# An FFT convolution with a SiLU feed-forward layer on one core: the inverse first stage as two half sums in four column quarters

## The chip, the cores and the metric

The kernel runs on one core of a Trainium2 chip, as one launch. The metric is the device time of that launch in microseconds (us). The core's engines have names of their own here: PE does the matmuls, PEld is its weight load, DVE, ACT and POOL do elementwise work, SP issues DMAs. PE writes to PSUM; DVE and ACT read PSUM or SBUF.

## The reference

Two functions follow each other. The first is a long causal convolution done by FFT, times its own input; the second is a feed-forward layer on each token.

```
h = (relu(pos_emb @ w1) @ w2) * exp(-0.01 * pos)[:, None]       # 12480 x 128
u = x * v                                                        # 2 x 12480 x 128
y = irfft(rfft(u, 24960) * rfft(h, 24960), 24960)[:, :12480]
a = x * y                                                        # tokens for the layer
g = a @ w_in;  g = g * sigmoid(g)                                # 24960 x 2048
out = g @ w_out                                                  # 24960 x 128
```

All inputs and outputs are f32.

## The kernel before

**The transform.** A sequence is taken as 2 x 98 x 64 positions: token 64 * (98 * i + t1) + t2, with i the half, t1 the slow index of 98 values and t2 the fast one of 64. The forward transform takes stage A over t1 (98 rows contracted against the constant `fa`) and stage B over t2 (`fb`, `fc`), two of the 98 values of k1 at a time. Products with the filter's spectrum follow, then the inverse of stage B, whose result `ws` goes to a DRAM tensor `wd`, as a real and an imaginary part for every k1 and t2. The inverse of stage A, which the change is about, is done in the second half of the kernel, tile by tile: y(t1, t2) is the sum over 98 values of k1 of real part times cosine and imaginary part times sine, with `fai` [98, 2, 98] as the constant.

**The stages in time.** The filter and batch 0 come first. Then the feed-forward loop runs over 52 token tiles. For its first 24 tiles batch 1 is transformed beside it, a side generator (`batch1_steps`) whose events the loop draws a few per step from a table of offsets; afterwards the loop runs alone.

**A token tile** is five values of t2 (the last tile of each half has four) with 97 or 98 values of t1 each, so 490, 486, 392 or 388 token columns. `load_tile` fetches the tile of `wd` (the two parts, 98 partitions) and the matching columns of x. `attn_tile` then does the inverse first stage. For each of the m values of t2, for both parts c and for both halves h of the 128 channels it issues one f32 matmul, which loads 64 columns of `wd` as weights and lets the 97 or 98 columns of `fai` pass (L656 to L665); the two parts accumulate in PSUM. DVE multiplies with x into `att` (L670), ACT rounds that to `ah` in the format fp32r (L671), DVE makes the rest `al` (L672). All matmuls of the layer use such pairs of a high and a low part, three products each.

**The loop** (L854 on) has 52 x 16 steps; a step is one block of 128 of the 2048 inner columns. On PE it does three hq matmuls (L861 to L863) and, for the step three before (LAG), three op matmuls (L889 to L891). Between lie silu on ACT (L868), gh on DVE or ACT (L870, L872) and gl on DVE (L873). hq has three PSUM buffers. While batch 1 runs beside, silu writes hq in place and gh and gl read it, so the buffer is free only after gl; later silu writes SBUF. The order on each engine is the order of the program text:

```
if f == 8 and n + 1 < len(tiles):
    attn[n + 1] = attn_tile(n + 1, *ahead.pop(n + 1), pmy, ("yp", 1))
if f == 9 and n + 2 < len(tiles):
    ahead[n + 2] = load_tile(n + 2)
while done < total and done * n_side < (s + 1) * total:
    done += next(side, total)
```

So in step 8 of a tile PE does the burst of L659 for the next tile, between hq of step 8 and op of step 5. ACT has ah and DVE has att and al in their queues between the work of steps 8 and 9. The burst's PSUM tile `yp` has one buffer and is written once per tile. Tile 0 is made ahead of the loop, with stage A groups of batch 1 around it (`seq3`, letter Y).

Of the kernel before, what the change touches and what calls it, by code (L numbers as in the profile page):

```python
# [10 lines left out]
F32 = mybir.dt.float32  # L11
# [3 lines left out]
ALU = mybir.AluOpType  # L15
# [8 lines left out]
D = 128  # L24
NJ = 64
DFF = 2048
R = 98
C = 64
T = R * C
N = 2 * T  # L30
NI = 2
NQ = R // 2
NF = DFF // 128


# [13 lines left out]
def tile_widths(i, n):  # L49

    if i == 0:
        return [98] * n
    w = [97] * n
    if n % 2:
        w[-1] = 98
    return w
# [28 lines left out]
def kernel(  # L85
# [17 lines left out]
    nc = tc.nc  # L103
# [9 lines left out]
    dram = dpool("dram")  # L113
    hs = dram.tile([NQ, 128, 512], F32, name="hs")
    wd = [dram.tile([R, NI, 128, D], F32, name=f"wd{b}") for b in range(NB)]

    const = pool("const")
    fa_sb = const.tile([R, 392], F32, name="fa_sb")
    fai_sb = const.tile([R, 2, R], F32, name="fai_sb")
    warm_sb = const.tile([1, 1], F32, name="warm_sb")  # L120
    win_sb = const.tile([R, 128], F32, name="win_sb")
    w1_sb = const.tile([128, 128], F32, name="w1_sb")
# [256 lines left out]
    for t in P["seq"]:  # L379
# [21 lines left out]
        elif t == "p":  # L401
            g = len(pts)
            pts.append(ppool.tile([128, NP, R], F32, name=f"pt{g}", tag="pt", bufs=8))
            for o in range(0, NP, 4) if g == 0 else [0]:
                n = 4 if g == 0 else NP
# [202 lines left out]

    for it in range(-1, NQ):
        if it + 4 < NQ:  # L610
            fbs[it + 4] = load_fb(rpa, it + 4, 7, nc.sync if it < 0 else nc.scalar, fc)
# [8 lines left out]
        if it >= 0:  # L620
            hab = habs.pop(it)
            at = products(it, up, hab[:, 1:2], "at", 3, nc.vector)
# [27 lines left out]
    def attn_tile(n, wt, xs, psp, tag):  # L650
        b, i, t2, m = tiles[n]
        ws = tile_widths(i, m)
        w = sum(ws)
        yp = psp.tile([128, 512], F32, name=f"yp{n}", tag=tag[0], bufs=tag[1])
        o = 0
        for t in range(m):  # L656
            for c in range(2):
                for h in range(0, D, 64):
                    nc.tensor.matmul(  # L659
                        yp[h : h + 64, o : o + ws[t]],  # L660
                        wt[:, c, t * D + h : t * D + h + 64],
                        fai_sb[:, c, 0 : ws[t]],
                        start=(c == 0),
                        stop=(c == 1),
                    )  # L665
            o += ws[t]
        at = mt.tile([128, 490], F32, name=f"att{n}", tag="att", bufs=1)
        ah = mt.tile([128, 512], F32R, name=f"ah{n}", tag="ah", bufs=2)
        al = mt.tile([128, 512], F32R, name=f"al{n}", tag="al", bufs=2)
        nc.vector.tensor_tensor(out=at[:, 0:w], in0=yp[:, 0:w], in1=xs[:, 0:w], op=ALU.mult)  # L670
        nc.scalar.copy(out=ah[:, 0:w], in_=at[:, 0:w])  # L671
        nc.vector.tensor_tensor(out=al[:, 0:w], in0=at[:, 0:w], in1=ah[:, 0:w].bitcast(F32), op=ALU.subtract)  # L672
        return ah, al
# [4 lines left out]
    for t in P["seq3"]:  # L678
# [13 lines left out]
        elif t == "U":  # L692
# [5 lines left out]
            mt = pool("mt")  # L698
# [31 lines left out]
    class Carved:  # L730


        at = dict(hab=(0,), at=(1024,), bt=(1792,), uw=(2560,), ws=(3072,), fb=(3584, 5868))
# [119 lines left out]
    op = {}  # L853
    for s in range(len(steps) + LAG):  # L854
        if s < len(steps):
            n, f = steps[s]
            w = sum(tile_widths(*tiles[n][1::2]))
# [7 lines left out]
            g = hp if beside else moe.tile([128, 490], F32, name=f"g{s}", tag="g", bufs=2)  # L865
# [15 lines left out]
        if s >= LAG:  # L881
            n, f = steps[s - LAG]
            w = sum(tile_widths(*tiles[n][1::2]))
            if f == 0:
                op[n] = pm.tile([128, 512], F32, name=f"op{n}", tag="op", bufs=2)
            o = op[n]
# [28 lines left out]
def _constants():  # L915
    k1 = np.arange(R, dtype=np.float64)
    t1 = np.arange(R, dtype=np.float64)
    t2 = np.arange(C, dtype=np.float64)
    k2 = np.arange(C, dtype=np.float64)
    phi = 2.0 * np.pi * np.outer(t1, k1 + 0.5) / 196.0  # L920
    alt = 1.0 - 2.0 * (np.arange(R) % 2)
    fa = np.concatenate([np.cos(phi), -np.sin(phi), alt * np.sin(phi), alt * np.cos(phi)], axis=1)
    fai = np.stack([np.cos(phi.T), -np.sin(phi.T)], axis=1) * (2.0 / N)
    th = 2.0 * np.pi * ((k1[:, None, None] + 0.5) / N + k2[None, None, :] / C) * t2[None, :, None]
    co, si = np.cos(th), np.sin(th)
    fwd = np.concatenate([np.concatenate([co, -si], axis=2), np.concatenate([si, co], axis=2)], axis=1)
    inv = fwd.transpose(0, 2, 1)
    fb = np.stack([fwd, inv], axis=1).reshape(NQ, 2, 2, 128, 128).transpose(0, 3, 1, 2, 4)
    rows_k2 = inv.reshape(NQ, 2, 2, 64, 128).transpose(0, 1, 3, 2, 4).reshape(NQ, 128, 2, 128)
    fc = np.stack([fwd.reshape(NQ, 2, 128, 128).transpose(0, 2, 1, 3), rows_k2], axis=2)  # L930
    pos = np.zeros(2 * T, np.float32)
    pos[:S] = np.arange(S, dtype=np.float32)
    win = np.exp(np.float32(-0.01) * pos)
    win = win.reshape(NI, R, C).transpose(1, 0, 2).reshape(R, 128)
    return {k: np.ascontiguousarray(a, dtype=np.float32) for k, a in dict(fa=fa, fai=fai, fb=fb, fc=fc, win=win).items()}


def _columns():

    cols = []  # L940
    for b, i, t2, n in token_tiles():
        for t, w in zip(range(t2, t2 + n), tile_widths(i, n)):
            tok = 64 * (R * i + np.arange(w)) + t
            cols.append(np.where(tok < S, b * S + tok, -1))
    return np.concatenate(cols)

# [40 lines left out]
```

## Time and profile before

| what | value |
|---|---|
| median of 3 runs | 1603.89 us (1602.04 to 1604.3) |
| the profiled execution | 1602.4 us, span 1600.6 us |
| granted clock of PE, mean | 0.994 |
| PE, DVE, ACT, POOL busy | 98%, 77%, 64%, 33% of the span |
| instructions | 30417 |

The span is what the profiler recorded; the execution's own time has 1.8 us around it. A PE instruction in the records is one pass: an f32 matmul makes two records, each with a weight load of its own. Matmuls are pipelined: the start of the next one comes before the end of the last, and the ends are modelled. "Idle before" in a row is the idle time of that engine just ahead of the instruction, and the arrow names what ended it.

### The profile page before, as it was taken

The page shows a single profiled execution, that of the slowest core. Times are in us where ns is not written, and L with a number is a line of the kernel's source. Part 1 is how long each engine was busy: PE and PEld are TensorE (multiplying, and loading weights), DVE is VectorE, ACT ScalarE, POOL GpSimd, SP SyncE. Part 2 cuts the span into 40 slices and gives each one's busy share as a digit, 9 for nine tenths or more (in the row PEclk, how much of TensorE's full clock was granted, in tenths as well). Part 3 has the DMA queues.
Part 4 walks back from the last instruction along what each step waited for, and adds up shares of the span by engine and source line. Part 5 has one row for each costly group of instructions (what it writes and reads, how often), then busy time and mean ns, then how long its engine had stood idle before and what let it go on. Part 6 is the DMA issues. An engine that isn't in the chain of part 4 may idle for free.

```text
span 1600.6 us, 30417 instructions
## 1 busy us (share of the span) xinstructions
PE 1569.5 (98%) x11372; PEld 1339.9 (84%) x11372; DVE 1235.3 (77%) x2028; ACT 1023.4 (64%) x1985; POOL 534.2 (33%) x520
## 2 busy tenths in 40 slices
PE   8979999899999999999999999999999999999999
PEld 7976666688888888988888888888888898888888
DVE  7567798555789998888888887777777777777776
ACT  3436676677777777777777765555555555555555
POOL 2456667423266666666666630000000000000000
PEclk9989999899999999999999999999999999999999
DMA  9477787744254555545545431111111111111110
GB/s 287 135 205 221 235 263 238 208 115 133 80 136 131 149 133 139 146 131 137 148 132 139 128 100 51 31 51 45 51 32 45 47 50 32 51 45 51 32 43 16
DMA packets 135564, 181.90 MB, mean 114 GB/s; under 512 B 10626, under 2 KB 78888, under 8 KB 135416
## 3 DMA queue, kind: packets, MB, share of 16 engines
q1 hardware_dynamic: 94392, 140.18, 30.9%
q10 hardware_dynamic: 40384, 37.67, 8.0%
q8 instruction: 90, 1.47, 0.4%
q0 software_dynamic: 640, 2.10, 0.4%
q14 instruction: 58, 0.48, 0.1%
HBM read 126.48 MB, written 53.42 MB: 112 GB/s over the span
## 4 chain that ended last, share of the span: by engine, by line
PE 93%; DVE 3%; DMA 2%; issue 1%; POOL 1%; ACT 0%; SPq 0%; ACTq 0%; POOLq 0%; DVEq 0%
PE op L889 12%; PE hq L862 11%; PE op L891 11%; PE hq L861 11%; PE op L890 11%; PE hq L863 11%; PE yp L659 6%; PE wp L601 3%; PE ap L236 2%; PE up L551 2%; PE wp L436 2%; PE up L436 2%; PE sp L568 2%; PE ap L209 2%; PE aph L209 1%
## 5 line engine op out<-in xcount | busy, mean ns | idle before, releaser
L868 ACT ACTIVATE g<-hq 128x486 f32<-128x486 f32 (+3 forms) x448 | 255.8, 571 | 223.8 <-PE hq L863 215.0
L873 DVE TENSOR_TENSOR gl<-g,gh 128x486 fp32r<-128x486 f32 (+3 forms) x448 | 294.5, 657 | 94.5 <-PE hq L863 59.2
L889 PE MATMUL op<-gh,woh 128*128 128x490 f32 (+3 forms) x832 | 323.4, 389 | 0.0
L861 PE MATMUL hq<-ah,wih 128*128 128x490 f32 (+3 forms) x832 | 315.8, 380 | 0.0
L862 PE MATMUL hq<-al,wih 128*128 128x490 f32 (+3 forms) x832 | 315.8, 380 | 0.0
L891 PE MATMUL op<-gh,wol 128*128 128x490 f32 (+3 forms) x832 | 315.4, 379 | 0.0
L863 PE MATMUL hq<-ah,wil 128*128 128x490 f32 (+3 forms) x832 | 315.1, 379 | 0.0
L890 PE MATMUL op<-gl,woh 128*128 128x490 f32 (+3 forms) x832 | 315.1, 379 | 0.0
L873 DVE TENSOR_TENSOR gl<-hq,gh 128x490 fp32r<-128x490 f32 (+2 forms) x384 | 251.7, 662 | 31.8 <-ACT gh L872 21.5
L868 ACT ACTIVATE hq<-hq 128x490 f32<-128x490 f32 (+2 forms) x384 | 214.1, 559 | 93.9 <-PE hq L863 65.5
L870 DVE CAST gh<-hq 128x490 fp32r<-128x490 f32 (+2 forms) x288 | 189.1, 657 | 49.8 <-ACT hq L868 48.3
L870 DVE CAST gh<-g 128x486 fp32r<-128x486 f32 (+3 forms) x336 | 137.8, 410 | 56.8 <-ACT g L868 54.7
L861 PEld LDWEIGHTS hq<-ah,wih 128*128 128x128 f32 x832 | 156.7, 188 | 25.5 <-DVE gl L873 0.8
L862 PEld LDWEIGHTS hq<-al,wih 128*128 128x128 f32 x832 | 156.6, 188 | 25.1 <-DVE al L672 0.2
L889 PEld LDWEIGHTS op<-gh,woh 128*128 128x128 f32 x832 | 156.5, 188 | 24.9
L891 PEld LDWEIGHTS op<-gh,wol 128*128 128x128 f32 x832 | 156.3, 188 | 25.0
L863 PEld LDWEIGHTS hq<-ah,wil 128*128 128x128 f32 x832 | 156.7, 188 | 24.4
L890 PEld LDWEIGHTS op<-gl,woh 128*128 128x128 f32 x832 | 156.5, 188 | 19.7 <-DVE gl L873 0.3
L659 PEld LDWEIGHTS yp<-fai_sb,slots 98*64 98x64 f32 x2048 | 89.3, 138 | 19.6 <-issue 16.4
L659 PE MATMUL yp<-fai_sb,slots 98*64 98x98 f32 (+1 forms) x2048 | 99.4, 252 | 2.3 <-DMA slots<-wd 2.3
L671 ACT CAST ah<-att 128x490 fp32r<-128x490 f32 (+3 forms) x52 | 30.9, 595 | 90.5 <-DVE att L670 90.5
L586 POOL TENSOR_TENSOR bt<-us,hab 128x512 f32<-128x512 f32 x49 | 65.3, 1333 | 64.3 <-ACT us L559 59.2
(1063 smaller groups left out, 2362.1 us busy)
## 6 DMA issues: line engine op xcount, KB each, us to landing
slots<-hs SPq DMA_DIRECT2D x98, 256.0 KB
slots<-wd SPq DMA_DIRECT2D x48, 490.0 KB
hs<-hab SPq DMA_DIRECT2D x49, 256.0 KB
wd<-ws SPq DMA_DIRECT2D x49, 256.0 KB
slots<-in_fb_dram SPq DMA_DIRECT2D x49, 256.0 KB
wd<-slots ACTq DMA_DIRECT2D x49, 256.0 KB
fb<-in_fc_dram ACTq DMA_DIRECT2D x45, 256.0 KB
xs<-in_x_dram SPq DMA_DIRECT2D x32, 196.0 KB
```

The lines of the kernel that those rows point to most:

```text
L436: nc.tensor.matmul(out[:, k].rearrange("p i d -> p (i d)"), f[:, k], a[:, k], start=(i == 0), stop=(i == len(passes) - 1),)
L586: e.tensor_tensor(out=t[:, 0:2].rearrange("p c (i d) -> p c i d", i=NI), in0=u, in1=h0.unsqueeze(2).broadcast_to([128, 2, NI, D]), op=ALU. ...
L659: nc.tensor.matmul(yp[h : h + 64, o : o + ws[t]], wt[:, c, t * D + h : t * D + h + 64], fai_sb[:, c, 0 : ws[t]], start=(c == 0), stop=(c = ...
L861: nc.tensor.matmul(hp[:, 0:w], wih[:, fs], ah[:, 0:w], start=True, stop=False)
L862: nc.tensor.matmul(hp[:, 0:w], wih[:, fs], al[:, 0:w], start=False, stop=False)
L863: nc.tensor.matmul(hp[:, 0:w], wil[:, fs], ah[:, 0:w], start=False, stop=True)
L868: nc.scalar.activation(out=g[:, 0:w], in_=hp[:, 0:w], func=AF.Silu)
L870: nc.vector.tensor_copy(gh[:, 0:w], g[:, 0:w])
L873: nc.vector.tensor_tensor(out=gl[:, 0:w], in0=g[:, 0:w], in1=gh[:, 0:w].bitcast(F32), op=ALU.subtract)
L889: nc.tensor.matmul(o[:, 0:w], woh[:, fs], gh[:, 0:w], start=(f == 0), stop=False)
L890: nc.tensor.matmul(o[:, 0:w], woh[:, fs], gl[:, 0:w], start=False, stop=False)
L891: nc.tensor.matmul(o[:, 0:w], wol[:, fs], gh[:, 0:w], start=False, stop=(f == NF - 1))
```

## The change

It uses a symmetry of the cosine and sine around t1 = 49. For every t2 two sums over k1 are made, y1 and y2, at 50 values j = 0 to 49. Their sum is y at t1 = 49 - j and their difference y at t1 = 49 + j. For that the host's tables are changed: `fai` becomes [98, 2, 50], and the inverse of stage B delivers the difference and the sum of the former two parts, swapped for odd k1, at the same size. The two sums no longer accumulate into each other, so each matmul starts and stops by itself; y1 lies in the first half of the PSUM tile, y2 in the second. The weights are 32 columns of `wd` in place of 64, so each matmul writes 32 partitions: four quarters h in place of two halves. A tile of five has 40 matmuls of 50 columns in place of 20 of 97 or 98.

New work follows: ACT copies y2 to SBUF (`s2`), DVE makes y1 + y2 (m x 50 columns) and y1 - y2 (m x 48 or m x 47 columns), and, in tiles of 486 columns, one more column alone. Then `att` is multiplied in place with x as before. The token columns of a tile stand in another order, for x and the output alike, and the host's column list follows.

```
--- before.py
+++ after.py
@@ -30,6 +30,7 @@
 N = 2 * T
 NI = 2
 NQ = R // 2
+HT = R // 2 + 1
 NF = DFF // 128
 
 
@@ -116,7 +117,7 @@
 
     const = pool("const")
     fa_sb = const.tile([R, 392], F32, name="fa_sb")
-    fai_sb = const.tile([R, 2, R], F32, name="fai_sb")
+    fai_sb = const.tile([R, 2, HT], F32, name="fai_sb")
     warm_sb = const.tile([1, 1], F32, name="warm_sb")
     win_sb = const.tile([R, 128], F32, name="win_sb")
     w1_sb = const.tile([128, 128], F32, name="w1_sb")
@@ -651,23 +652,37 @@
         b, i, t2, m = tiles[n]
         ws = tile_widths(i, m)
         w = sum(ws)
-        yp = psp.tile([128, 512], F32, name=f"yp{n}", tag=tag[0], bufs=tag[1])
-        o = 0
+
+        yp = psp.tile([128, 2, 256], F32, name=f"yp{n}", tag=tag[0], bufs=tag[1])
         for t in range(m):
             for c in range(2):
-                for h in range(0, D, 64):
+                for h in range(0, D, 32):
                     nc.tensor.matmul(
-                        yp[h : h + 64, o : o + ws[t]],
-                        wt[:, c, t * D + h : t * D + h + 64],
-                        fai_sb[:, c, 0 : ws[t]],
-                        start=(c == 0),
-                        stop=(c == 1),
+                        yp[h : h + 32, c, t * HT : (t + 1) * HT],
+                        wt[:, c, t * D + h : t * D + h + 32],
+                        fai_sb[:, c],
+                        start=True,
+                        stop=True,
                     )
-            o += ws[t]
         at = mt.tile([128, 490], F32, name=f"att{n}", tag="att", bufs=1)
         ah = mt.tile([128, 512], F32R, name=f"ah{n}", tag="ah", bufs=2)
         al = mt.tile([128, 512], F32R, name=f"al{n}", tag="al", bufs=2)
-        nc.vector.tensor_tensor(out=at[:, 0:w], in0=yp[:, 0:w], in1=xs[:, 0:w], op=ALU.mult)
+        s2 = mt.tile([128, 256], F32, name=f"s2{n}", tag="s2", bufs=1)
+        nc.scalar.copy(out=s2[:, 0 : m * HT], in_=yp[:, 1, 0 : m * HT])
+        y1, y2 = (a[:, 0 : m * HT].rearrange("p (t j) -> p t j", t=m) for a in (yp[:, 0], s2))
+        o, r = m * HT, ws[0] - HT
+        nc.vector.tensor_tensor(out=at[:, 0:o].rearrange("p (t j) -> p t j", t=m), in0=y1, in1=y2, op=ALU.add)
+        nc.vector.tensor_tensor(
+            out=at[:, o : o + m * r].rearrange("p (t j) -> p t j", t=m),
+            in0=y1[:, :, 1 : 1 + r],
+            in1=y2[:, :, 1 : 1 + r],
+            op=ALU.subtract,
+        )
+        if w > o + m * r:
+            nc.vector.tensor_tensor(
+                out=at[:, w - 1 : w], in0=y1[:, m - 1, HT - 2 : HT - 1], in1=y2[:, m - 1, HT - 2 : HT - 1], op=ALU.subtract
+            )
+        nc.vector.tensor_tensor(out=at[:, 0:w], in0=at[:, 0:w], in1=xs[:, 0:w], op=ALU.mult)
         nc.scalar.copy(out=ah[:, 0:w], in_=at[:, 0:w])
         nc.vector.tensor_tensor(out=al[:, 0:w], in0=at[:, 0:w], in1=ah[:, 0:w].bitcast(F32), op=ALU.subtract)
         return ah, al
@@ -920,11 +935,18 @@
     phi = 2.0 * np.pi * np.outer(t1, k1 + 0.5) / 196.0
     alt = 1.0 - 2.0 * (np.arange(R) % 2)
     fa = np.concatenate([np.cos(phi), -np.sin(phi), alt * np.sin(phi), alt * np.cos(phi)], axis=1)
-    fai = np.stack([np.cos(phi.T), -np.sin(phi.T)], axis=1) * (2.0 / N)
+
+
+    ph = phi[HT - 1 :: -1].T
+    g = np.stack([np.cos(ph) + np.sin(ph), np.cos(ph) - np.sin(ph)], axis=1) / N
+    fai = np.where((np.arange(R) % 2 == 0)[:, None, None], g, g[:, ::-1])
     th = 2.0 * np.pi * ((k1[:, None, None] + 0.5) / N + k2[None, None, :] / C) * t2[None, :, None]
     co, si = np.cos(th), np.sin(th)
     fwd = np.concatenate([np.concatenate([co, -si], axis=2), np.concatenate([si, co], axis=2)], axis=1)
     inv = fwd.transpose(0, 2, 1)
+    minus, plus = inv[:, :, :C] - inv[:, :, C:], inv[:, :, :C] + inv[:, :, C:]
+    even = (np.arange(R) % 2 == 0)[:, None, None]
+    inv = np.concatenate([np.where(even, minus, plus), np.where(even, plus, minus)], axis=2)
     fb = np.stack([fwd, inv], axis=1).reshape(NQ, 2, 2, 128, 128).transpose(0, 3, 1, 2, 4)
     rows_k2 = inv.reshape(NQ, 2, 2, 64, 128).transpose(0, 1, 3, 2, 4).reshape(NQ, 128, 2, 128)
     fc = np.stack([fwd.reshape(NQ, 2, 128, 128).transpose(0, 2, 1, 3), rows_k2], axis=2)
@@ -939,8 +961,9 @@
 
     cols = []
     for b, i, t2, n in token_tiles():
-        for t, w in zip(range(t2, t2 + n), tile_widths(i, n)):
-            tok = 64 * (R * i + np.arange(w)) + t
+        t1 = [np.arange(HT)[::-1]] * n + [np.arange(HT, w) for w in tile_widths(i, n)]
+        for t, a in zip([*range(t2, t2 + n)] * 2, t1):
+            tok = 64 * (R * i + a) + t
             cols.append(np.where(tok < S, b * S + tok, -1))
     return np.concatenate(cols)
```

## Rows read from the trace of the kernel before

**Rows 1.** Page, part 1: busy us (share of span) xinstructions

```profile
PE 1569.5 (98%) x11372; PEld 1339.9 (84%) x11372; DVE 1235.3 (77%) x2028; ACT 1023.4 (64%) x1985; POOL 534.2 (33%) x520
```

**Rows 2.** Page, part 4: chain that ended last, by engine and by line

```profile
PE 93%; DVE 3%; DMA 2%; issue 1%; POOL 1%; ACT 0%; SPq 0%; ACTq 0%; POOLq 0%; DVEq 0%
PE op L889 12%; PE hq L862 11%; PE op L891 11%; PE hq L861 11%; PE op L890 11%; PE hq L863 11%; PE yp L659 6%; PE wp L601 3%; PE ap L236 2%; PE up L551 2%; PE wp L436 2%; PE up L436 2%; PE sp L568 2%; PE ap L209 2%; PE aph L209 1%
```

**Rows 3.** Windows: length, busy PE, PEld, DVE, ACT, POOL; PE clock, DMA share, GB/s

```profile
690.00:820.00 130.00, 130.00 (x816) 112.99 (x815) 115.31 (x183) 99.09 (x194) 83.11 (x87) 1.00 0.51 135
...
1100.00:1250.00 150.00, 150.00 (x898) 127.29 (x897) 109.54 (x195) 82.85 (x143) 0.00 (x0) 1.00 0.15 44
```

**Rows 4.** Timeline of PE around one burst: start us, us, engine, line, operation

```profile
709.08 1.90 PE L659 MATMUL yp<-fai_sb,slots 98*64 98x97 f32 x40
710.91 0.48 PE L889 MATMUL op<-gh,woh 128*128 128x486 f32 x1
```

**Rows 5.** Groups by line: xcount | busy us, mean ns of one | idle before

```profile
L659 PEld LDWEIGHTS yp<-fai_sb,slots 98*64 98x64 f32 x2048 | 89.3, 138 | 19.6 <-issue 16.4
L659 PE MATMUL yp<-fai_sb,slots 98*64 98x98 f32 (+1 forms) x2048 | 99.4, 252 | 2.3 <-DMA slots<-wd 2.3
...
L236 PEld LDWEIGHTS ap<-fa_sb,slots 98*128 98x128 f32 x240 | 41.6, 194 | 6.4 <-POOL slots L264 2.5 <-issue 2.1
```

**Rows 6.** Timeline of PE and PEld, 709.00 to 709.13: what of the burst had started

```profile
709.08 0.30 PE L659 MATMUL yp<-fai_sb,slots 98*64 98x97 f32 x2
...
709.08 0.14 PEld L659 LDWEIGHTS yp<-fai_sb,slots 98*64 98x64 f32 x2 [0.34 <-issue]
```

**Rows 7.** A full-width group of L236: timeline; its sequencer's waits, ns min/median/max, first and last start

```profile
293.11 1.56 PE L236 MATMUL ap<-fa_sb,slots 98*128 98x196 f32 x8
...
L236 PEldq EVENT_SEMAPHORE  x2: 51/1140/2229, 293.0 to 293.1; - x2
```

**Rows 8.** Instructions of L670 and L873: ns min/median/max, first and last start, forms

```profile
L670 DVE TENSOR_TENSOR att<-yp,slots x52: 555/665/670, 303.9 to 1567.9; 128x490 f32<-128x490 f32 x24, 128x486 f32<-128x486 f32 x24, 128x392 f32<-128x392 f32 x2, 128x388 f32<-128x388 f32 x2
...
L873 DVE TENSOR_TENSOR gl<-hq,gh x384: 555/666/672, 310.2 to 962.2; 128x490 fp32r<-128x490 f32 x96, 128x486 fp32r<-128x486 f32 x88, 128x392 fp32r<-128x392 f32 x8
```

**Rows 9.** Instructions of L468 on DVE (from PSUM) and L771 on ACT, 256 columns

```profile
L468 DVE TENSOR_TENSOR slots<-up,slots x49: 414/415/418, 436.0 to 939.4; 128x256 f32<-128x256 f32 x49
...
L771 ACT CAST fw0h<-slots x1: 406/406/406, 427.6 to 427.6; 128x256 fp32r<-128x256 f32 x1
```

**Rows 10.** Timeline behind the burst of rows 4: DVE, ACT, the third next hq

```profile
711.27 0.66 DVE L873 TENSOR_TENSOR gl<-hq,gh 128x486 fp32r<-128x486 f32 x1
711.84 0.65 DVE L670 TENSOR_TENSOR att<-yp,slots 128x486 f32<-128x486 f32 x1
713.16 0.67 DVE L672 TENSOR_TENSOR al<-att,ah 128x486 fp32r<-128x486 f32 x1 [0.67 <-ACT ah L671]
...
714.63 0.67 DVE L873 TENSOR_TENSOR gl<-hq,gh 128x486 fp32r<-128x486 f32 x1
...
712.53 0.60 ACT L671 CAST ah<-att 128x486 fp32r<-128x486 f32 x1 [2.19 <-DVE att L670]
...
716.35 0.38 PE L861 MATMUL hq<-ah,wih 128*128 128x486 f32 x1
```

**Rows 11.** Timeline in two other tiles: gl of step 9, the third next hq

```profile
585.89 0.67 DVE L873 TENSOR_TENSOR gl<-hq,gh 128x490 fp32r<-128x490 f32 x1
...
586.98 0.38 PE L861 MATMUL hq<-ah,wih 128*128 128x490 f32 x1
...
637.76 0.67 DVE L873 TENSOR_TENSOR gl<-hq,gh 128x490 fp32r<-128x490 f32 x1
...
640.16 0.38 PE L861 MATMUL hq<-ah,wih 128*128 128x490 f32 x1
```

**Rows 12.** Timeline in the second kind: gl of step 9, its op

```profile
1408.62 0.67 DVE L873 TENSOR_TENSOR gl<-g,gh 128x486 fp32r<-128x486 f32 x1
...
1411.48 0.38 PE L890 MATMUL op<-gl,woh 128*128 128x486 f32 x1
```

## Prediction

> **What bounds the kernel now.** I read the busy shares first: PE is busy 98% of the span, DVE 77%, ACT 64% [rows 1]. The chain that ended last says the same in another way: 93% of it is PE, and 6% of the span is the line that the change rewrites, L659 [rows 2]. A share is an average, so the stages come next: two stretches show the two kinds that follow the first 306 us [rows 3]. Up to about 962 us the second batch is transformed beside the feed-forward loop: PE is busy for the whole 130 us of the stretch, DVE for 89% of it, ACT for 76%. Afterwards POOL has nothing left, DVE is at 73%, and PE still has no gap. So a microsecond of PE work that goes is a microsecond gained, as long as DVE keeps its appointments; in the first kind of stretch it has 11% of the time to spare.
>
> Each of the 52 tiles has one burst of L659. The one shown [rows 4] lasts 1.90 us, and op follows at 710.91. It holds 40 records for 20 matmuls, since each f32 matmul makes two. A record ends 0.25 us after its start [rows 5], so 20 pairs of records took about 1.65 us, 82.5 ns a pair. That two halves of the array run together is visible twice. The first two weight loads fill 0.14 us together, which is the length of one, and two matmuls have started within 50 ns of the burst's begin [rows 6]. And a matmul over the full width with 196 columns takes 1.56 us for eight records [rows 7]; less the last one's 0.33 that is 1.23 over seven gaps, 176 ns each, 0.90 ns a column. A pair of L659, 97 columns in each half, costs 0.85 ns a column. So one half costs what the whole width would, and two go for the price of one.
>
> **The change, part by part.** *The burst.* A tile of five now issues 5 x 2 x 4 = 40 matmuls, 80 records, of 50 columns each and 32 wide. If four quarters go together, 20 groups at 50 x 0.85 = 42.5 ns remain; I take 44 for a fixed part that I can't separate, so 0.88 us for 1.65, and 0.77 saved. A tile of four saves 0.62. The first tile's burst I count at nothing: the first hq behind it waits for the DVE chain, which gets longer by about what the burst saves. Of the other 51 tiles 47 are of five and four of four [rows 8]: 47 x 0.77 + 4 x 0.62 = **38.7 us saved**. No row shows four quarters. The bounds are this value (the columns must pass, so nothing lies far below it) and every record at today's 41 ns, 80 x 41 = 3.3 us, which is 84 us lost over 51 tiles. I take the low end because the two things that could prevent it have room by the nearest rows. Weight loads last 138 ns at 64 wide and 194 at 128 [rows 5], 0.87 ns a column, so 28 ns go for 32 columns, under the 42.5 of the matmul that covers it. Issue: eight instructions per 44 ns are wanted, 5.5 ns each; the sequencer came to its next wait at 293.1, when the first matmul of the sixteen instructions ahead of that wait had just started [rows 7], some 6 ns an instruction.
>
> One rule speaks against it. In the rows two halves start within a few ns of each other [rows 6], yet nothing in them keeps a pace under 41 ns a record. The Trainium skill (TensorE: Matmul & The Clock Gate, section Back-to-back issue gap) puts a floor of about 25 ns on the distance of two matmul starts, however few the columns. By that 80 records take 2.0 us, an estimate, and the sum would end near 1622.
>
> *The DVE work.* A sum over 250 columns, a difference over 235 or 240, and in the 24 tiles of 486 columns a third instruction on one column. The row for 128x256 is 415 ns [rows 9], so 0.41 and 0.40 busy. In a full queue an instruction of 0.66 is followed 0.57 after its start [rows 10], so each costs some 0.09 less: 0.32 + 0.31, and 0.06 for the small one half of the time, 0.66 us in all; twice 0.41 and 0.15 make 0.97 the upper bound. The multiply stays as long as it was: it reads SBUF alone now, and al, of the same size and from SBUF alone, takes 0.67 where att from PSUM takes 0.65 [rows 10].
>
> *The ACT copy* of 250 columns takes at most 0.41, the row for 256 [rows 9]. It waits for the burst; behind it in ACT's queue are ah and the next silu. ACT idles 2.19 us there waiting for att, and DVE is still at gl when the copy is done [rows 10], so it is counted at nothing; in a tile without that idle time it is 0.4 us on the chain. The smaller constant is loaded long before its first use; columns of x and out change their order on the host; yp and the copy's one buffer are free some 20 us before the next burst.
>
> *What is late next.* Behind the burst DVE does add, subtract, multiply, waits 0.67 for ah, then al, gh, gl. In the first kind of stretch (24 tiles, 384 steps in which gl reads hq itself [rows 8]) hq has three buffers, so the third next hq needs this gl. In the tile shown gl ends at 715.30 and that hq starts at 716.35: 1.05 us to spare [rows 10]. The change takes 0.77 of it (PE is earlier) and 0.66 (DVE is later), 1.43 together. Two other tiles have 0.42 and 1.73 [rows 11]. PE would stall 1.0, 0.4 and 0 us: about 0.5 on average, over 24 tiles **12 us given back**; the bounds are 0 and 1.43 each, 34 us. In the second kind gl ends at 1409.29 and the op that needs it starts at 1411.48 [rows 12]: 2.19 less 1.43 leaves 0.8, and no stall.
>
> *The sum.* The profiled execution took 1602.4 us: 1602.4 - 38.7 + 12 = 1575.7. The median of the runs stands 1.5 above it: **1577**.
>
> **The rivals.** *A, slower: only two quarters run at once*, by a limit of the read path. Then 40 pairs at 44 ns are 1.76 us, 0.11 x 51 = 6 us more, and the DVE work adds perhaps 1 us of stalls: 1609 to 1611. For it: no row has four. Against it: the second half costs nothing today.
> *B, slower or same: every record keeps a distance from the last*, hidden today under 41 ns. At half of that, 20.6 ns, the burst is as long as now, and with 2 us of DVE stalls the time is 1606; from there on each further ns is 80 x 51 = 4 us. The page's 25 ns belongs here. At 41 ns it is 1688; that the quarters simply stay one behind another, and the change doesn't do what it says, is this end.
> *C, no stall.* Slips spread over DVE's spare 11%: 1565. For it: PE waits nowhere now. Against it: the tiles with little to spare.
> *D, DVE saturates.* A tile of the first kind lasts 652 us / 24 = 27 us [rows 8], of which DVE has 3 free, and 1.43 go. If all of that turns into waiting in 24 tiles, 34 us come back: 1599.
> *E, four quarters overlap, but loading or feeding sets the pace*, say 60 ns a group: 1.2 us a burst, 0.45 x 51 = 23 saved, 6 given back: 1587.
>
> **How the numbers follow.** My forecast 0.52, A 0.10, B 0.09, C 0.12, D 0.09, E 0.08. A measurement of this kernel can tell 0.2%, 3.2 us, from no change. Faster takes the forecast, C, E and most of D: 0.78; same a little of B and D, 0.04; slower 0.18. The likeliest case alone is 1568 to 1588. The range reaches past C below and over D to the near edge of B above, 1560 to 1606, and leaves out A and most of B.
>
> **What would show it.** Right: a burst of about 1.1 us with 80 records and four weight loads within some 25 ns of each other; two new groups on DVE of about 0.40; PE idle behind step 9 of a tile with gl as the releaser, before 962 us only, some 12 us in all. A or B show as a burst of 1.9 us or more, C as no PE wait, D as waits in most steps of the first kind. The forecast is wrong if bursts last over 1.3 us or PE's waits pass 20 us.

## The result, and the profile after

The median is 1586.46 us over 4 runs (1585.18 to 1586.65), against 1603.06 us for the kernel before, timed beside it: ratio 0.9896, 95% interval 0.988 to 0.9911. The forecast was 1577, so the sign and the range held, and the size was off by 9.5 us. The profiled execution took 1586.4 us, span 1584.5.

First the page of the kernel after: busy times, and the chain that ended last.

```profile
PE 1544.3 (97%) x13420; PEld 1302.0 (82%) x13420; DVE 1262.3 (80%) x2156; ACT 1029.9 (65%) x2037; POOL 531.7 (34%) x520
...
PE 80%; DVE 8%; ACT 4%; issue 3%; DMA 3%; POOL 2%; ACTq 0%; SPq 0%; DVEq 0%; POOLq 0%
PE hq L876 10%; PE op L904 10%; PE hq L878 10%; PE hq L877 10%; PE op L906 10%; PE op L905 10%; PE wp L602 3%; PE yp L660 2%; PE up L552 2%; PE ap L237 2%; PE sp L569 2%; PE up L437 2%; DVE gl L888 1%; PE wp L437 1%; PE aph L210 1%
```

PE lost 25 us of busy time [rows 1], but the span only 16: PE now waits. The burst's line fell from 6% of the chain to 2%, and DVE and ACT hold 12% of it where they held 3% [rows 2]. The windows of [rows 3] say in which stage (columns as there):

```profile
690.00:820.00 130.00, 128.51 (x945) 109.09 (x943) 118.47 (x197) 100.49 (x200) 82.83 (x86) 1.00 0.50 139
1100.00:1250.00 150.00, 150.00 (x1197) 126.08 (x1196) 115.74 (x215) 85.79 (x153) 0.00 (x0) 1.00 0.16 45
```

PE has gaps in the first kind of stretch and none in the second. The waits between 450 and 950 us, first of the kernel before, then of the one after (us in total, times, longest us):

```profile
ACT ah L671 <- DVE att L670: 28.5, 18, 2.5
DVE al L672 <- ACT ah L671: 11.9, 18, 0.7
...
PEld hq L861 <- DVE gl L873: 0.3, 1, 0.3
```

```profile
ACT ah L686 <- DVE att L685: 39.4, 19, 3.0
PEld hq L876 <- DVE gl L888: 14.8, 30, 1.3
DVE al L687 <- ACT ah L686: 12.6, 19, 0.7
...
PE hq L876 <- DVE gl L888: 4.7, 9, 0.9
```

The new wait on PE's side is the one that was foreseen, hq for gl. The change's own instructions, of the kernel after (ns min/median/max, first and last start, forms):

```profile
L660 PEld LDWEIGHTS yp<-fai_sb,slots x4096: 106/109/174, 301.9 to 1551.5; 98*32 98x32 f32 x196
L660 PE MATMUL yp<-fai_sb,slots x4096: 205/207/291, 301.9 to 1551.6; 98*32 98x50 f32 x196
L671 ACT COPY s<-yp x52: 327/370/377, 304.2 to 1551.8; 128x250 f32<-128x250 f32 x48, 128x200 f32<-128x200 f32 x4
L674 DVE TENSOR_TENSOR att<-yp,s x52: 355/410/419, 304.6 to 1552.7; 128x250 f32<-128x250 f32 x48, 128x200 f32<-128x200 f32 x4
...
L682 DVE TENSOR_TENSOR att<-yp,s x24: 145/148/149, 665.4 to 1530.8; 128x1 f32<-128x1 f32 x24
```

And the timeline of the same tile as in [rows 4, 10]:

```profile
713.06 1.10 PE L660 MATMUL yp<-fai_sb,slots 98*32 98x50 f32 x80
714.09 0.48 PE L904 MATMUL op<-gh,woh 128*128 128x486 f32 x1
714.22 0.37 ACT L671 COPY s<-yp 128x250 f32<-128x250 f32 x1
...
714.85 0.38 PE L876 MATMUL hq<-ah,wih 128*128 128x486 f32 x1
...
715.80 0.41 DVE L674 TENSOR_TENSOR att<-yp,s 128x250 f32<-128x250 f32 x1
716.12 0.40 DVE L675 TENSOR_TENSOR att<-yp,s 128x235 f32<-128x235 f32 x1
...
716.62 0.67 DVE L685 TENSOR_TENSOR att<-att,slots 128x486 f32<-128x486 f32 x1
717.32 0.60 ACT L686 CAST ah<-att 128x486 fp32r<-128x486 f32 x1 [2.72 <-DVE att L685]
...
717.82 0.41 ACT L786 CAST iv26h<-slots 128x256 fp32r<-128x256 f32 x1
717.95 0.67 DVE L687 TENSOR_TENSOR al<-att,ah 128x486 fp32r<-128x486 f32 x1 [0.67 <-ACT ah L686]
...
718.13 0.55 ACT L883 ACTIVATE hq<-hq 128x486 f32<-128x486 f32 x1
...
718.72 0.67 DVE L885 CAST gh<-hq 128x486 fp32r<-128x486 f32 x1
...
719.41 0.67 DVE L888 TENSOR_TENSOR gl<-hq,gh 128x486 fp32r<-128x486 f32 x1
...
720.13 0.48 PE L876 MATMUL hq<-ah,wih 128*128 128x486 f32 x1 [0.46 <-DVE gl L888]
```

From the burst's start to op are 1.03 us, where it was 1.83: 0.80 gained. Then follow the loss line by line. The hq that began at 714.85 belongs to step 9, and its three matmuls end near 715.7. Its silu starts at 718.13, because ah stands ahead of it in ACT's queue and waits 2.72 us for the multiply; a cast of 0.41 for batch 1 comes between the two. On DVE, al waits 0.67 for ah, and gh of step 9 stands behind al; it starts at 718.72, when both al (718.62) and silu (718.68) have ended. gl ends at 720.08, and the third next hq, which needs that buffer, starts at 720.13 after a wait.

### The profile page after: what moved, and what is told of

It reads as the page before. It is cut to its first block, busy times and chain, and to the rows that moved or that the text cites. A ratio compares the mean times of both kernels' runs of the same rounds, so it can differ in the third digit from the quotient of the medians.

```text
span 1584.5 us, 34705 instructions
## 1 busy us (share of the span) xinstructions
PE 1544.3 (97%) x13420; PEld 1302.0 (82%) x13420; DVE 1262.3 (80%) x2156; ACT 1029.9 (65%) x2037; POOL 531.7 (34%) x520
## 4 chain that ended last, share of the span: by engine, by line
PE 80%; DVE 8%; ACT 4%; issue 3%; DMA 3%; POOL 2%; ACTq 0%; SPq 0%; DVEq 0%; POOLq 0%
PE hq L876 10%; PE op L904 10%; PE hq L878 10%; PE hq L877 10%; PE op L906 10%; PE op L905 10%; PE wp L602 3%; PE yp L660 2%; PE up L552 2%; PE ap L237 2%; PE sp L569 2%; PE up L437 2%; DVE gl L888 1%; PE wp L437 1%; PE aph L210 1%
## 5 line engine op out<-in xcount | busy, mean ns | idle before, releaser
L876 PE MATMUL hq<-ah,wih 128*128 128x490 f32 (+3 forms) x832 | 320.7, 385 | 6.4 <-DVE gl L888 5.3
L462 POOL TENSOR_TENSOR slots<-slots 128x512 f32<-128x512 f32 x49 | 63.5, 1295 | 61.5 <-ACT slots L456 61.5
L475 DVE TENSOR_TENSOR at<-at,bt 128x768 f32<-128x768 f32 x49 | 51.8, 1057 | 23.9 <-POOL bt L593 23.9
```

The source lines that it names most:

```text
L462: e.tensor_tensor(out=t[:, 0:2].rearrange("p k (i d) -> p k i d", i=NI), in0=u, in1=hab[:, :, m, 0].unsqueeze(2).broadcast_to([128, 2, NI, ...
L475: nc.vector.tensor_tensor(out=at, in0=at, in1=bt, op=ALU.add)
L876: nc.tensor.matmul(hp[:, 0:w], wih[:, fs], ah[:, 0:w], start=True, stop=False)
```

## The experiments

Each was timed beside the kernel before, whose median was 1602.9 to 1604.2 us.

**1. The burst alone.** The copy, sum and difference are taken out; the multiply reads yp directly.

```diff
-nc.scalar.copy(out=s2[:, 0 : m * HT], in_=yp[:, 1, 0 : m * HT])
...
+yf = yp.rearrange("p c n -> p (c n)")
+nc.vector.tensor_tensor(out=at[:, 0:w], in0=yf[:, 0:w], in1=xs[:, 0:w], op=ALU.mult)
```

> Edit: the changed kernel without ACT's copy and DVE's sum and difference; the burst of four quarters stays, DVE multiplies what it left with x. Left out: the two half sums are never combined, so the output isn't the reference's. Theory 1 (late gl): the DVE work behind the burst makes gl late, and PE's stalls for the free hq buffer eat what the burst saves in the first kind of stretch. Then 1563 to 1568 us (1602.4 less 39.7 of shorter bursts), tiles of the first kind near 26.0 us instead of 26.7, PE stalls for gl under 2 us in all. Rival 1 (another chain): POOL, the DMAs or ACT set the pace of the first kind of stretch as soon as PE gets faster. Then those tiles stay at 26.4 to 26.7 and the time is 1575 or more. On the slower matmuls of the second kind (222.8 ns from start to start for 490 columns instead of 220.0): this kernel has no s2 buffer, so SBUF addresses are those of before; theory P (place) says 220.0 again, theory Q (the engines' timing behind a shorter burst) says 222 to 223.

Measured: 1569.5 us (1568.66 to 1571.75), ratio 0.9795 [0.9776, 0.9815]. What stands behind the burst costs 17 us, and the burst by itself brings 33.4, less than 38.7. The time is 1.5 us above theory 1's range. The expectation took the addresses to be those of before. They were not, since the smaller constant moves the buffers in this kernel too, and its matmuls of 490 columns came 222.8 ns apart as in the kernel after; experiments 5 and 6 say what that costs.

**2. The sums alone.** The burst of the kernel before, with the copy, sum and difference of the change behind it (on columns of the old yp).

> Edit: the kernel before with its burst of two halves, and the changed kernel's ACT copy, sum and difference added behind it on columns of the old result. Left out: nothing of the work, but the sums are of the wrong values, so the output isn't the reference's. Theory 1: DVE is later by 0.66 us and PE is not earlier, the spare time of about 1 us covers most of it: 1603 to 1609 us. Rival 2 (DVE is a second bottleneck already): the added 0.8 us per tile is paid in full in the 24 tiles of the first kind, 1620 us or more. On the matmuls' pace: theory P says 222 to 223 ns and tiles of 490 columns in the second kind at 23.4 us instead of 23.17; theory Q says 220.0 and 23.17.

Measured: 1610.89 us, ratio 1.0048 [1.0033, 1.0063]. That is 1.9 us above theory 1's range and under rival 2's 1620. On the old burst the same work costs 8 us, on the new one 17; in the profiled executions, from the loop's first burst (burst 1) on, 5.5 and 12.6. The two parts don't add: the earlier PE and the later DVE eat the same spare time.

**3. One buffer more.** The kernel before with a buffer of 1 KB a partition in the place of s2.

```diff
+if n == 0:
+    pad = mt.tile([128, 256], F32, name="pad", tag="s2", bufs=1)
+    nc.gpsimd.memset(pad, 0.0)
```

> Edit: the kernel before with a buffer of 1 KB per partition in the place that s2 takes, written once and never used; all else is as before. Theory P (the s2 buffer moves gh, gl and what lies behind it in SBUF, and matmuls that read there get slower): 222 to 223 ns for 490 columns, tiles of 23.4 us in the second kind, 1607 to 1610 us in all. Theory Q: 220.0 ns, 23.17 us, 1602 to 1604 us.

Measured: 1603.18 us, ratio 1.0 [0.999, 1.0009]. It was run because the loop's matmuls had become slower in the stretch without any wait; a KB more is not why.

**4. The new work spread over steps.** The kernel after, with the copy and the sum in step 8, the difference in 9, the multiply in 10, ah in 11, al in 12. The loads of x and of the tile of `wd` move from step 9 to 11.

```diff
-attn[n + 1] = attn_tile(n + 1, *ahead.pop(n + 1), pmy, ("yp", 1))
+parts = attn_tile(n + 1, *ahead.pop(n + 1), pmy, ("yp", 1))
+attn[n + 1] = next(parts)
...
+elif f > 8 and n + 1 < len(tiles):
+    next(parts, None)
```

> Edit: the changed kernel with the work behind the burst spread over steps 8 to 12: copy and sum in step 8, difference in 9, multiply in 10, ah in 11, al in 12; x and the next tile are loaded in step 11 instead of 9. Theory 1: no step has to wait for all of it, gl is on time, and most of the 11 us of stalls come back: 1572 to 1578 us, tiles of the first kind near 26.2. Rival 1: 1584 to 1588, as with the work in one place. If the load two steps later is too late, PE waits for it at the burst, some 1 us a tile, and the time is over 1590.

Measured: 1583.09 us (1581.33 to 1584.26), ratio 0.9877 [0.9857, 0.9896]. Its waits between 450 and 950 us:

```profile
ACT ah L689 <- DVE att L687: 20.4, 18, 2.3
PEld hq L883 <- DVE gl L895: 17.3, 33, 1.2
```

Theory 1 failed: PE waits for gl no less than in the kernel after. The 3.4 us in the medians are no proof of a gain: in the profiled executions this one is 3.1 us ahead already when burst 1 starts (321.62 against 324.69). ah is one step behind the multiply here and still waits 20.4 us for it, with silu of step 12 behind it: over tiles 5 to 23 that silu starts 1.33 us behind its hq on average, where those of steps 9 to 11 start 0.04 to 0.08 behind. On DVE gh of step 13 stands behind al, and in 13 of the 19 tiles it starts right at al's end; on average it comes 0.81 behind its silu. PE's delays moved with it, from the hq of step 12 to those of step 14 and of the next tile's step 0. So the spread moved the hold-up to later steps, and this run does not say which of the two queues makes it.

**5. The old places.** The kernel after with the constant's buffer kept at its old size of 98 x 2 x 98, so that all later buffers keep their old places, but for the KB of experiment 3.

```diff
-fai_sb = const.tile([R, 2, HT], F32, name="fai_sb")
+fai_sb = const.tile([R, 2, R], F32, name="fai_sb").rearrange("p c n -> p (c n)")[:, 0 : 2 * HT].rearrange("p (c n) -> p c n", c=2)
```

> Edit: the changed kernel with the smaller constant in a buffer of the old size, so that all that lies behind it in SBUF stands where it stood before (the s2 buffer's 1 KB aside). The instructions are the same. Theory P2 (the matmuls that read ah, al, gh, gl and the weights got slower because the constant's buffer shrank by 384 bytes and moved them all by 384): 220.0 ns from start to start for 490 columns instead of 222.8, tiles of the second kind at 22.35 us instead of 22.61 and at 22.35 instead of 22.46, 1579 to 1583 us in all. Theory Q (it is the four quarters in the array, or the engines' timing behind a shorter burst): 222.8 ns and 22.61 us as before this edit, 1584 to 1588 us.

Measured: 1578.36 us (1577.08 to 1579.14), ratio 0.9846 [0.9831, 0.9861]: 8.1 us less than the kernel after, with the same instructions, and 0.6 under theory P2's range. One line of hq's matmuls in the second kind of stretch, 1100 to 1250 us (ns min/median/max), in the kernels before, after and of this run:

```profile
L862 PE MATMUL hq<-al,wih x103: 382/382/383, 1100.2 to 1249.2; 128*128 128x490 f32 x103
```

```profile
L877 PE MATMUL hq<-al,wih x106: 384/386/388, 1100.4 to 1249.2; 128*128 128x490 f32 x106
```

```profile
L877 PE MATMUL hq<-al,wih x108: 382/382/383, 1100.0 to 1249.9; 128*128 128x490 f32 x108
```

In 150 us the kernel after does 106 where this one does 108. From start to start a matmul of 490 columns takes 222.8 ns in the kernel after and 220.0 before and here. That is a mean over the layer's six lines: five take 223.0 to 224.6 in the kernel after, the op line that reads gl takes 218.0. The constant shrank by 384 bytes a partition, and that moved ah, al and the split weights of `w_out` 384 bytes down, and gh and gl 640 up (with s2's KB between). The split weights of `w_in` kept their place.

**6. The same shift in the kernel before.** 640 bytes a partition ahead of the weights of `w_out` and the token buffers bring them to the kernel after's places modulo 1 KB.

```diff
+shift = mw.tile([128, 160], F32, name="shift")
+nc.gpsimd.memset(shift, 0.0)
```

> Edit: the kernel before with a buffer of 640 bytes per partition ahead of the layer's second weights, written once and never used. It puts those weights, ah, al, gh and gl at the same distance from a multiple of 1024 bytes as in the changed kernel, and gh and gl at the same addresses. The instructions of PE are the same as before. Theory P2: 222 to 223 ns for 490 columns, tiles of the second kind at 23.4 us instead of 23.17 (490 columns) and at 23.25 instead of 23.15 (486), 1606 to 1612 us. Theory Q: 220.0 ns, 23.17 us, 1601 to 1605 us.

Measured: 1610.18 us (1606.65 to 1610.47), ratio 1.0037 [1.0024, 1.005]. Nothing but places changed, and 7 us are lost; the matmul of 490 columns again takes 222.8 ns. So the places are a cost of the change that has nothing to do with its computation. Which buffer matters, and why, is open.

**7 and 8. Less work for DVE.** gh goes to ACT in every third step in place of every fourth while batch 1 runs beside, in the kernel of experiment 5 and in the kernel before.

```diff
-fp=4,
+fp=3,
```

> Edit: the kernel of the run e5 (old places), and in the first kind of stretch gh of steps 0, 3, 6, 9, 12, 15 on ACT instead of 0, 4, 8, 12: two of sixteen go from DVE to ACT, step 9 behind the burst among them. Theory 1 in its later form (DVE's load as a whole, not its bunching, makes gl late): DVE has 1.3 us less per tile of the first kind, stalls for gl nearly go, tiles of the first kind near 25.8 us instead of 26.4, and the time is 10 to 14 us under that of e5. Rival 3 (the chain over ACT: silu waits in ACT's queue behind ah): ACT gets 1.1 us more per tile, the stalls stay or grow, the time is within 3 us of e5 or above it.

> Edit: the kernel before, with gh of steps 0, 3, 6, 9, 12, 15 on ACT in the first kind of stretch as in e7. By theory 1 PE has no stalls there to give back, so it changes nothing: 1601 to 1605 us, tiles of the first kind at 26.5 us. If DVE's load bounded the kernel before as well, it would be faster by more than 5 us.

Measured: 1594.88 us, ratio 0.9951 [0.9934, 0.9968]; and 1605.51, ratio 1.0018 [1.0008, 1.0027]. The waits of the first, 450 to 950 us:

```profile
ACT ah L686 <- DVE att L685: 51.4, 19, 3.2
...
DVE gl L888 <- ACT gh L887: 30.3, 48, 1.5
PEld hq L876 <- DVE gl L888: 27.9, 43, 1.7
```

The first is 16.5 us above experiment 5, where theory 1 had it 10 to 14 under; the second is 2.4 us above the kernel before and just over the range. DVE is busy for 430.9 of those 500 us, less than in the kernel before (445.7), and PE waits longer than ever. So DVE's load as a whole is not what makes gl late. gh of step 9 is on ACT in this run: over tiles 5 to 23 it starts 0.03 us behind silu on average and gl 0.03 behind gh, and still the third next hq starts only 0.14 behind gl's end. Here ACT alone holds gl up: silu starts 2.55 behind its hq.

**9. The late split.** The kernel of experiment 5, with ah issued in step 10, behind that step's silu, gh and gl, and al in step 11. The burst, copy, sums and multiply stay in step 8; not an instruction is removed.

```diff
 nc.vector.tensor_tensor(out=at[:, 0:w], in0=at[:, 0:w], in1=xs[:, 0:w], op=ALU.mult)
+yield ah, al
 nc.scalar.copy(out=ah[:, 0:w], in_=at[:, 0:w])
+yield
 nc.vector.tensor_tensor(out=al[:, 0:w], in0=at[:, 0:w], in1=ah[:, 0:w].bitcast(F32), op=ALU.subtract)
-return ah, al
+yield
...
+if f in (10, 11) and n + 1 < len(tiles):
+    next(parts)
```

> The changed kernel with its buffers at the old places, and the split of the token tile moved: the copy ah is issued in step 10 behind that step's silu, gh and gl, the difference al in step 11; the copy s2, the sum, the difference and the multiply stay in step 8. Theory (ACT's queue blocks: ah waits for the multiply, which is now later, silu of step 9 stands behind ah, and gh and gl of step 9 come late): silu of step 9 now runs ahead of ah, the 15 us in which the matmuls of step 9 on wait for gl between 450 and 950 us fall to 5 or less, the tiles of the first kind of stretch fall from 26.37 to about 25.9 us, and the time to 1565 to 1570 us. Rival (VectorE's own work is what delays gl, whatever stands in ACT's queue): the waits stay at 12 to 17 us, a tile at 26.3 to 26.4 us, the time at 1576 to 1580 us. If ah in step 10 only pushes the same blocking two steps on, silu of step 11 waits instead and the time is also 1576 or more.

Measured: 1565.05 us (1564.31 to 1565.87), ratio 0.9757 [0.9741, 0.9773]. Its waits, 450 to 950 us:

```profile
DVE gl L893 <- ACT gh L892: 5.0, 13, 0.8
...
PEld hq L881 <- DVE gl L893: 4.3, 14, 0.7
...
ACT ah L687 <- DVE att L685: 0.6, 2, 0.4
```

And its timeline, in the same tile as above:

```profile
701.96 0.39 PE L881 MATMUL hq<-ah,wih 128*128 128x486 f32 x1
...
702.82 0.56 ACT L888 ACTIVATE hq<-hq 128x486 f32<-128x486 f32 x1 [0.82 <-PE hq L883]
...
703.74 0.73 DVE L685 TENSOR_TENSOR att<-att,slots 128x486 f32<-128x486 f32 x1
...
704.39 0.65 DVE L890 CAST gh<-hq 128x486 fp32r<-128x486 f32 x1
704.61 0.59 ACT L687 CAST ah<-att 128x486 fp32r<-128x486 f32 x1
...
705.08 0.67 DVE L893 TENSOR_TENSOR gl<-hq,gh 128x486 fp32r<-128x486 f32 x1
...
706.63 0.38 PE L881 MATMUL hq<-ah,wih 128*128 128x486 f32 x1
```

The silu of step 9 starts as soon as its hq is done, with ah behind it; gl ends 0.88 before the third next hq. DVE does as much as in experiment 5 (1265.2 against 1259.1 us busy) and PE hardly waits. This is the fastest version that computes the whole reference, 38.9 us under the kernel before.

**10. The multiply on GpSimd**, ah in step 11 and al in step 12, otherwise as experiment 9.

```diff
-nc.vector.tensor_tensor(out=at[:, 0:w], in0=at[:, 0:w], in1=xs[:, 0:w], op=ALU.mult)
+nc.gpsimd.tensor_tensor(out=at[:, 0:w], in0=at[:, 0:w], in1=xs[:, 0:w], op=ALU.mult)
```

> The same kernel with the multiply by the gate on GpSimd instead of VectorE, ah in step 11 and al in step 12. Theory (ACT's queue blocks, VectorE's load comes second): as the run before or a little better, since VectorE loses some 0.6 us a tile: 1562 to 1569 us. Rival 1 (VectorE's own work delays gl): this takes from VectorE about what the sum and the difference add less a little, so the waits for gl fall in this run and not in the run before: 1568 to 1573 us against 1576 to 1580. Rival 2 (GpSimd, about two thirds busy in the first kind of stretch, becomes late with its side work or with the multiply, so that ah and the output matmuls wait): 1572 us or more, with waits for GpSimd that are not there in the run before.

Measured: 1594.3 us (1594.23 to 1596.7), ratio 0.9944 [0.993, 0.9959], far above the theory's figure: the rival with GpSimd took place.

```profile
POOL att L685 <- DVE att L682: 32.2, 10, 4.2
POOL att L685 <- DVE att L675: 16.8, 5, 5.0
PEld hq L881 <- DVE gl L893: 14.6, 30, 1.7
...
PEld up L437 <- POOL xs22l L797: 2.7, 1, 2.7
```

It is the same fault on a third queue: the multiply stands at the head of GpSimd's queue and waits for the sums (up to 5 us), the work of batch 1 stands behind it, and PE waits for that.

**11. The late split in the kernel before**, the control.

> The kernel before with ah moved to step 10 and al to step 11 in the same way: the control. Theory: the kernel before has next to no wait for gl to give back (0.3 us between 450 and 950 us), so nothing changes: 1601 to 1605 us. If the late split by itself is worth time, whatever the change does, this run is faster by as much as the first run of this call is faster than 1578 us; if it does harm (the output matmuls wait for ah or al), it is over 1607 us.

Measured: 1603.7 us, ratio 1.0001 [0.9991, 1.001]. The late split is worth nothing where gl has time to spare.

**12. The burst alone, in the old places**: experiment 1 with the buffer of experiment 5.

> The closing account: the changed kernel with its buffers at the old places and without the copy s2, the sum, the difference and the one column; the multiply reads the first w values of yp, so t1's two sums are not combined and the output is not the reference's; ah and al stay in step 8. Theory (the burst and the places are all that is left once nothing is added behind the burst): 1569.5 less the 8 us of the moved buffers, 1560 to 1564 us, a tile of the first kind at 25.8 to 25.9 us; the version with the late split, at 1565.05 us, then has taken back all but 1 to 5 us of what the sums cost. Rival (the late split brought a gain of its own beyond the price of the sums): this run is at 1566 us or more. If places and sums are not separate terms, it is under 1558 us.

Measured: 1562.45 us (1561.09 to 1564.58), ratio 0.9747 [0.9731, 0.9763]. The late split is 2.6 us above it, so in the medians it has taken back all but that of what the sums cost in experiment 5 (15.9). In the profiled executions the two take the same time from burst 1 on, 1236.9 and 1237.2 us; what differs lies ahead of it.

## Why the prediction was right in part

The account goes by the starts of bursts in the timelines of the profiled executions (us between them; "last" is the last op matmul):

| stretch | before | after | exp. 5, old places | exp. 9, late split | exp. 12, burst only, old places |
|---|---|---|---|---|---|
| burst 0 starts at | 300.28 | 301.86 | 300.95 | 300.82 | 298.97 |
| burst 0 to 1 | 21.49 | 22.83 | 21.99 | 22.64 | 19.42 |
| burst 1 to 5 | 123.27 | 124.48 | 123.63 | 120.01 | 120.55 |
| burst 5 to 25 | 527.62 | 524.79 | 524.02 | 513.96 | 513.70 |
| burst 25 to last | 624.21 | 606.83 | 602.91 | 602.92 | 602.92 |

From burst 1 to the end, before to experiment 12 is what the burst brings, 12 to 5 the price of the sums, 5 to after that of the places: -37.9 + 13.4 + 5.5 us. Ahead of burst 1 the kernel after is 2.9 us later. Together that is -16.1, the difference of the two last starts. The forecast had -38.7 + 12 = -26.7. That the time still lies in the range is owed to the range's width: of the 10.6 us between the two, 5.5 are the price of the places, which the sum did not have.

The -37.9 is not the burst's term of the forecast yet: the shorter burst alone makes PE wait for gl already. Taken from each burst's first matmul to the op behind it, the 51 bursts from burst 1 on last 92.3 us before and 51.8 in the kernel after and in experiments 5, 9 and 12: 40.5 saved. All the rest of PE's time from burst 1 on is 2.6 us longer than before in experiment 12, 5.5 in experiment 2 and 16.0 in experiment 5. Term by term, with the buffers in their old places, that is -40.5 + 16.0 for the forecast's -38.7 + 12.

**The burst: right.** 40.5 for 38.7. A tile of 490 columns in the second kind fell by 0.8 us (23.17 to 22.35 in experiment 12), where 0.77 was forecast. The quarters run together: 16 weight loads and 12 matmuls had started in the burst's first 0.14 us, in this view of the kernel after, PEld and PE from 713.00 to 713.20:

```profile
713.06 0.25 PEld L660 LDWEIGHTS yp<-fai_sb,slots 98*32 98x32 f32 x16 [0.34 <-issue]
...
713.06 0.34 PE L660 MATMUL yp<-fai_sb,slots 98*32 98x50 f32 x12
```

In a burst of the kernel after, four records start within 20 ns. Of the 20 groups the second starts some 69 ns after the first, and each later one on average 44.8 ns after the one before it, where I took 44. A, B and E are out. The floor of about 25 ns between matmul starts that the Trainium skill states (TensorE: Matmul & The Clock Gate, section Back-to-back issue gap) would have made this burst 2.0 us long, an estimate from the page's figure. The row has 80 records in 1.10, so the floor doesn't hold for matmuls in different column quarters.

**The stall: the place was right, the size a third too low, the path not whole.** 16.0 us for 12. The two shifts draw on one stock of spare time: 2.6 and 5.5 us apart, 16.0 together. In tiles 5 to 23 of experiment 5 a step's first hq starts later behind the matmul before it than the usual 0.22: 7.2 us in sum at step 12, whose hq needs gl of step 9 (at most 1.12 in one tile), and 0.6 at all other steps; beyond 965 us PE waits for gl nowhere. The second kind pays nothing for the sums (602.91 against 602.92). The forecast counted two shifts against the spare time, 0.77 for PE and 0.66 for DVE, 1.43 in all, and that held: gl of step 9 comes 1.51 later against its hq than before (1.26 less 0.13 of the table below, and 0.38 a tile of waiting). What was low is the average of three tiles, 0.5 us a tile. The rest of the order it took as given. Step 9 over the same 19 tiles, means in us:

| | silu starts behind its hq's end | gh starts behind silu's end | third next hq starts behind gl's end |
|---|---|---|---|
| before | 0.49 | 0.12 | 1.26 |
| exp. 12, burst only | 1.24 | 0.14 | 0.55 |
| exp. 5, burst and sums | 2.04 | 0.14 | 0.13 |
| exp. 9, late split | 0.04 | 0.75 | 1.12 |

The sentence that failed is the one on ACT: it named ah and the next silu behind the copy, took ACT's 2.19 us of idle time [rows 10] as cover, and counted ACT at nothing, with a chain over DVE alone: multiply, ah, al, gh, gl. The copy itself is covered: it ends at 714.59 and DVE comes to the sum at 715.80. But that idle time is not spare. It is ah, at the head of an in-order queue, holding back a silu whose hq is ready. So a later multiply delays silu as well: by 0.80 from experiment 12 to 5. al, which waits 0.67 for ah, stands ahead of gh on DVE too, but mostly it is not the last: in experiment 5 it ends 0.32 before silu's end on average, and earlier in 14 of the 19 tiles. Experiment 9 takes both out of the way; experiment 7 shows that ACT's queue alone is enough. DVE's alone was not tried. C (no stall) did not happen in the kernel after; the late split reaches its figure, 1565. D fell with experiments 7 and 9.

**Missed: the places.** The forecast had the smaller constant "loaded long before its first use" and said nothing of what lies behind it. Its 384 bytes cost 5.5 us from burst 1 on, 3.9 of them in the second kind, and 7 to 8 us in the medians of experiments 5 and 6.

**Open in part: the 2.9 us ahead of burst 1.** 1.6 are there before burst 0, whose start scatters from 298.97 to 302.27 over all fourteen profiles, with the sums and without. Behind burst 0, in the kernel after, PE waits 1.1 us for ah and al:

```profile
307.37 0.77 PE L876 MATMUL hq<-ah,wih 128*128 128x490 f32 x1 [0.71 <-ACT ah L686]
308.56 0.78 PE L877 MATMUL hq<-al,wih 128*128 128x490 f32 x1 [0.41 <-DVE al L687]
```

Experiments 1 and 12, the same burst without the sums, have no such wait; that part belongs to the change, and the forecast had counted the first tile at nothing. The rest of burst 0 to 1 follows the granted clock from 300 to 312 us, which is at the lower of its two levels, 1.2 GHz, for all of the stretch in the kernel after and for part of it in the others: mean 0.50 in the kernel after, 22.83 us; 0.57, 21.99 (experiment 5); 0.65, 21.49 (before); 0.81, 19.42 (experiment 12). Ahead of burst 0 PE had waited for a DMA, 3.21, 1.12, 2.27 and 1.73 us in these four. The kernel of experiment 11, which is the one before up to there, had a wait of 0.64, a clock of 1.00 and 19.06 us, so much of it differs from run to run. But the seven kernels with the sums take 21.99 to 23.63 us from burst 0 to 1 and the seven without them 19.06 to 22.12, so how much of the 2.9 is the change's stays open.

## What to carry to other kernels

Idle time of an engine ahead of an instruction that waits is not spare time: whatever stands behind that instruction is held up too (2.04 us for silu in experiment 5, 0.04 in experiment 9). So look at what is next in that queue before a producer is made later, and let consumer and producer stand far enough apart: two steps did it in experiment 9, one was not enough in experiment 4. A gain on PE and a delay on the engine that feeds it draw on the same spare time, and are to be set against it together (2.6 and 5.5 us apart, 16.0 together). And when a buffer changes its size, keep the places of those behind it, or time both.

## What the runs showed of the hardware that was not expected

Matmuls that load 32 columns each and write four quarters of the partitions start 6 to 7 ns apart within a group, and behind the first one a group of four f32 records of 50 columns takes 44.8 ns. Weight loads took 110 ns on average at 32 columns, where 64 took 138 and 128 took 194 [rows 5]. And the place of SBUF buffers changed the pace of long matmuls: 222.8 ns in place of 220.0 for 490 columns in experiment 6, where nothing but places was changed, by 640 bytes. A move of gh and gl by 1024 bytes (experiment 3) left it at 220.0.
